# mLSTM cell and quick-gelu MLP on one core: the second product of the last chunk as three float32r products of 12-bit parts

## The chip, the cores and the metric

The kernel runs on one core of a Trainium2 chip. The metric is device time in microseconds of one launch, the median of several runs. Beside it there is one profiled execution with a trace of every instruction: its span is the time from the first instruction to the last. Engines are named as in the profile: PE (matmul) and PEld (its weight load), DVE (VectorE), ACT (ScalarE), POOL (GpSimd), SP (the queue that issues most DMAs).

## The reference, cut to what matters

The first part is an mLSTM recurrence over 768 steps for 4 batches and 8 heads of 40. Its output, turned to 3072 tokens by 320, goes through an MLP with 2048 hidden units:

```python
def _moe_ref(x, w_in, w_out) -> np.ndarray:      # x 3072 x 320
    h = x @ w_in                                  # w_in 320 x 2048
    g = h * (1.0 / (1.0 + np.exp(-1.702 * h)))
    return (g @ w_out).astype(np.float32)         # w_out 2048 x 320
```

Inputs and output are fp32.

## The kernel before

**Chunks.** The sequence is cut into NW = 6 chunks w of 128 steps. A chunk has 4 batches, so 512 tokens. For each chunk the kernel computes the recurrence in chunked form (`attention`, L967), then the first product with gelu, then the second product. The order of instructions is written out by hand in the loop over w (from L980); each engine takes its instructions in that order, and waits only for data and for buffers. While PE works on chunk w's second product, the recurrence of chunk w + 1 is put between its blocks through the table `side`.

**First product.** Chunk 0 uses plain fp32 (`up`, L645). Chunks 1 to 5 use `up_fast` (L789): inputs and weights are split into 12-bit parts, named high, low, diff and rest, and eight float32r matmuls of 128x128 by 512 tokens are summed for each of two hidden slices, j = 0 to 7. Four go to a bank called side, four to one called main. ACT copies side out of PSUM with a factor (L823), DVE joins main to it (L825), and ACT takes the gelu in place (L784) one j later. The result `gs[w, j]` holds 2 slices of 128 hidden units by 512 tokens. Even j take PSUM from two pairs of banks (`banks`, L356), odd j from four single ones.

The weight parts `w_diff` and `w_low` do not all fit in SBUF. In chunk 1 they are made and written to DRAM by `keep` (L728, on ACT's queue), and later chunks bring them back with `fetch_diff` and `fetch_low` (L749 to L754, on SP's queue) in the last blocks of the chunk before.

**Second product.** Chunk 0 uses `down` (L830): 64 fp32 matmuls with gelu outputs of 128 tokens as weights and 320 columns of `w_out` moving. Chunks 1 to 5 use `down_fast` (L876), one level of Strassen's scheme (Winograd's form) in fp32: two blocks of 128 tokens by the two halves of the hidden units by the two halves of the columns. There are 7 products of 8 matmuls with 160 columns for each of two pairs of token blocks, so 14 blocks of code and 112 matmuls (L889) instead of 64 with 320 columns. The token side needs sums of gelu outputs: `hidden_difference` and `hidden_sums` (L854 to L868, POOL and DVE) and `last_sums` (L870, DVE). The weight side needs `t1`, `t2`, `t4` and w11 - w01; `weight_sums` (L846, POOL) makes them once, and the last one overwrites `w01`, the right half of the first eight slices of `w_out_sb` (L93), in chunk 1 (L1035). DVE folds each product into the output tile (L892, L894), and SP stores it (L898).

**The loop's places that matter here.** In the loop over j of a chunk w > 0 (L1011 to L1053) each `up_fast(w, j)` is followed by `keep` and the weight splits (chunk 1), the next chunk's loads and transposes, `hidden_difference` from j = 2 or 3 on, and `hidden_sums` on POOL for j = 6 and 7. Then come the last gelu and `hidden_sums(w, (2, 3), V)` (L1057), and the blocks of the second product (L1065). In the last chunk there is no next chunk, so ACT, DVE and POOL have only the gelu chain and the sums.

Of the kernel before, what the change touches and what calls it, by code (L numbers as in the profile page):

```python
# [18 lines left out]
L = 128  # L19
# [12 lines left out]
def kernel(  # L32
# [44 lines left out]


    f_sb, i_sb = {}, {}
    k_st = const.tile([L, BH * D + DP - D], FP, name="k_st")  # L80
    q_sq = const.tile([L, BH // 2 * 4 * D + 32], FP, name="q_sq")
    k_sq = const.tile([L, BH // 2 * 4 * D + 32], FP, name="k_sq")
    t_sb = const.tile([128, 3, NH * DH], FP, name="t_sb")
    t1, t2, t4 = (t_sb[:, i, :].rearrange("p (f m) -> p f m", m=DH) for i in range(3))
    t_flat = t_sb.rearrange("p i x -> p (i x)")
    q_st, k_0, k_1 = (t[:, 0:BH * DP].rearrange("s (h d) -> s h d", d=DP) for t in (q_sq, k_sq, t_flat))
    at_bits, at_const = BH * DP, BH * DP + 1024
    v_st = const.tile([L, BH, D1], FP, name="v_st")
    eo = {}
    w_in = [win.tile([128, 2, 512], FP, tag="wa", name="w_in") for _ in range(3)]  # L90
    w_in.append(work.tile([128, 2, 512], FP, tag="wx", bufs=1, name="w_in"))
    w_in_x = work.tile([128, NF // 2, 128], FP, tag="xh", bufs=1, name="w_in_x")
    w_out_sb = const.tile([128, NF, DM], FP, name="w_out_sb")  # L93

    def load_gates(w):
        for dst, src in ((f_sb, f_gate), (i_sb, i_gate)):
# [43 lines left out]
    w_out_flat = w_out_sb.rearrange("p f m -> p (f m)")  # L140


    def piece_in(c, n):
# [7 lines left out]
    def piece_out(n):  # L151
        parts, c = [], n * 512
        while c < n * 512 + 512:
            f, m = divmod(c, DM)
            e = min(c + DM - m, n * 512 + 512)
            parts += [(slice(0, 128), slice(c - n * 512, e - n * 512), out_bits[:, f, 2 * m:2 * (m + e - c)])]
            c = e
        return w_out_flat[:, n * 512:(n + 1) * 512], parts

    pieces = []  # L160
    for n in range(4):
# [67 lines left out]
        G.memset(t[:, :, D:DP], 0.0)  # L229

    mark = const.tile([L, 1], FP, name="mark")
    state = [const.tile([128, BH // 2, D1], FP, name=f"state{i}") for i in range(2)]
    state_mid = const.tile([128, BH // 2, D1], FP, name="state_mid")

    m_at, ends = {0: m0}, {}
# [385 lines left out]
    def wait_for(x):  # L621

        G.tensor_copy(out=mark[0:x.shape[0]], in_=x[:, 0:1])
# [206 lines left out]
    def down(w, b, n):  # L830
        if n == 0:
            o_ps[w, b] = ps_m.tile([128, DM], FP, tag="m", name="p_out")
        po = o_ps[w, b]
        for f in range(n * 4, n * 4 + 4):
            T.matmul(po, gs[w, f // 2][:, f % 2, b * L:(b + 1) * L], w_out_sb[:, f, :], start=(f == 0),  # L835
                     stop=(f == NF - 1))
# [6 lines left out]
    w00, w01 = w_out_sb[:, 0:NH, 0:DH], w_out_sb[:, 0:NH, DH:DM]  # L843
    w10, w11 = w_out_sb[:, NH:NF, 0:DH], w_out_sb[:, NH:NF, DH:DM]
# [31 lines left out]
    def down_fast(w, c):  # L876
# [19 lines left out]
        def store(two):  # L896
# [8 lines left out]
                lambda: (product(block(1, 1), t4, (o10, o10)), store(1)),  # L905
                lambda: (product(total(2), w11, (o01, o01)), store(0))]


    def run(calls):
        for f, *args in calls:  # L910
            f(*args)
# [68 lines left out]
    for w in range(NW):  # L980
        more = w + 1 < NW
        if w == 0:
            for j in range(NF // 2):
                if j % 2 == 0:
                    ahead, behind = converted[j // 2]
                    if j:
                        run([(convert, p) for p in ahead])
                    run([(fetch, p) for p in fetched.get(j // 2, ())])
                    up(w, j, lambda: run([(columns_turn, 1) if p is None else (convert, p) for p in behind]), last_seam)
                if j == 6:  # L990
                    load(1, "o")
                if j == 1:
                    wait_for(w_in[1][:, 1, :])
                    scale(0, 1)
                    load(1, "v")
                if j < B and j % 2:
                    carry(0, j // 2)
                if j == 3:
                    masks()
                    gates(1)  # L1000
                    columns_in(1)
                if j == 4:
                    spread(1)
                    load_squares(1, "q")
                if j >= B:
                    transposes(1, j - B)
        else:
            if w == 1:
                split_diff(1)
                split_low(1, V)  # L1010
                more_rooms(1)  # L1011
            for j in range(NF // 2):
                up_fast(w, j)
                if more and j == 0:
                    gates(w + 1)
                if w == 1:
                    if j == 0:
                        split_high(2)
                    if j == 1:
                        for n in (0, 1):  # L1020
                            keep(w_diff_row, n, w_diff[1, n])
                        split_diff(2)
                        split_low(2, V)
                    if j == 2:
                        split_high(3)
                        keep(w_diff_row, 2, w_diff[1, 2])
                        keep(w_low_row, 2, w_low[1, 2])
# [21 lines left out]
                lag = 3 if w == 1 else 2  # L1049
                if lag <= j < 4 + lag:  # L1050
                    hidden_difference(w, j - lag)
                if j >= 6:
                    hidden_sums(w, (j - 6,), G)  # L1053
            gelu_fast(w, NF // 2 - 1)
            if more:
                load(w + 1, "o")
            hidden_sums(w, (2, 3), V)  # L1057
        side = attention(w + 1) if more else {}
        if more:
            rooms(w + 1)  # L1060
        if w == 0:

            blocks = [(lambda b=b, n=n: down(w, b, n)) for n0 in (0, 2) for b in range(B) for n in (n0, n0 + 1)]
        else:
            blocks = down_fast(w, 0) + down_fast(w, 1)  # L1065
        for i, block in enumerate(blocks):
            if w == 0 and i == 0:
                columns(1)
                convert_begin(17)
                weights_exp(1, 0)  # L1070
                fill_squares(q_sq)
                convert_end(17)
                for n in (1, 3, 5, 7):
                    block_transposes(1, n)
            if w == 0 and i in (4, 5):
                convert(14 + i)
            if w + 2 < NW and i == (6 if w == 0 else 0):
                load_gates(w + 2)
            if w == 0 and i == 13:
                load_squares(w + 2, "k")  # L1080
            if w == 0 and i == 15:
                load_squares(w + 2, "q")
            block()
            run(side.get(i, []))
            if w == 1 and i == 4:
                last_sums(1, 0, (2, 3))
            if w == 0 and i == 5:
                wait_for(w_out_flat[:, 9 * 512:])
                weight_sums(1)
                weight_sums(3)  # L1090
            if w == 0 and i == 5:
                split_high(0)
                split_rest()
                split_high(1)
            if w == 0 and i == 9:
                split_diff(0)
                split_low(0, V)
                split_rest_low()
            if w and more:
                if i == 11:  # L1100
                    fetch_diff(w + 1, (0, 1))
                    fetch_low(w + 1)
                    if w + 2 < NW:
                        load_squares(w + 2, "k")
                if i == 13:
                    fetch_diff(w + 1, (2, 3))
                    if w + 2 < NW:
                        load_squares(w + 2, "q")

# [29 lines left out]
```

## Time and profile before

| | us |
|---|---|
| three runs | 445.94, 448.19, 444.94 |
| median | 445.94 |
| the profiled execution's own time | 447.5 |
| its span | 445.8 |
| PE busy in it | 440.1 |
| last chunk, first product (chain, from 382.91) | 29.38 |
| last chunk, second product (chain, from 412.29) | 30.44 |
| from its end at 442.73 to the end of the span | 3.1 |

Times inside the span count from its start. In the chain of work that ended last, each piece is a start, a length, an engine, what it wrote, a line of the kernel and the number of records. A matmul in fp32 leaves two records in the trace, one in float32r leaves one. PE's records overlap, so the spacing of starts, or a piece's length over its count, tells what a matmul costs; the length of one record is longer.

### The profile page before, as it was taken

How to read it: one execution, taken by the hardware profiler on the slowest of the kernel's cores; microseconds unless marked ns; L12 is line 12 of the kernel's file. 1: busy time of each engine (PE TensorE's matmuls, PEld its weight loads, DVE VectorE, ACT ScalarE, POOL GpSimd, SP SyncE). 2: the span in 40 equal slices, each digit the busy share in tenths (PEclk: the TensorE clock that was granted, in tenths of full speed). 3: DMA queues.
4: the chain of work that ended last, by engine and by line, in shares of the span. 5: the costliest groups of instructions: out<-in, count | busy, mean ns of one | idle time of the engine just before them, and what ended most of it. 6: DMA issues, size and time to landing. Idle time of an engine off the chain costs nothing.

```text
span 445.8 us, 12211 instructions
## 1 busy us (share of the span) xinstructions
PE 440.1 (99%) x4999; PEld 384.0 (86%) x4999; DVE 327.3 (73%) x660; ACT 228.9 (51%) x494; POOL 130.8 (29%) x131
## 2 busy tenths in 40 slices
PE   8999999999999999999999999999999999999997
PEld 6867887776889999888999888999888999888997
DVE  4888999989999877778686779686769566634512
ACT  5677779902787701687701486800486900366000
POOL 6401327440066700135700034700035610035000
PEclk9999999999999999999999999999999999999999
DMA  8999999017777427979026978216988306600000
GB/s 168 196 283 165 242 271 216 2 35 196 183 200 161 63 63 218 267 111 168 13 59 188 270 102 176 44 34 143 328 114 156 61 19 151 232 31 0 1 31 29
DMA packets 129656, 60.06 MB, mean 135 GB/s; under 512 B 102096, under 2 KB 122528, under 8 KB 129600
## 3 DMA queue, kind: packets, MB, share of 16 engines
q1 hardware_dynamic: 120512, 54.86, 55.8%
q10 hardware_dynamic: 8768, 4.28, 3.3%
q8 instruction: 39, 0.64, 0.6%
q0 software_dynamic: 320, 0.15, 0.2%
q14 instruction: 17, 0.14, 0.1%
HBM read 49.10 MB, written 10.16 MB: 133 GB/s over the span
## 4 chain that ended last, share of the span: by engine, by line
PE 93%; SPq 4%; DMA 2%; DVE 1%; issue 0%; ACT 0%; DVEq 0%
PE p_out L889 34%; PE p L806 17%; PE p_h L806 16%; PE p_out L835 8%; PE p_h L657 7%; SPq L132 3%; PE p L534 2%; PE p L490 2%; PE p L542 2%; PE p L633 2%; PE p_h L666 2%; DMA bits<-in_moe_w_in_dram 2%; DVE state L610 0%; PE p L406 0%; DVE state_mid L642 0%
## 5 line engine op out<-in xcount | busy, mean ns | idle before, releaser
L857 POOL TENSOR_TENSOR g<-g 128x512 f32<-128x512 f32 x20 | 25.8, 1297 | 159.5 <-ACT g L784 159.5
L889 PE MATMUL p_out<-w_out_sb,g 128*128 128x160 f32 x480 | 68.9, 300 | 0.0
L889 PEld LDWEIGHTS p_out<-w_out_sb,g 128*128 128x128 f32 x480 | 66.4, 190 | 0.6
L765 ACT ACTIVATE x_high<-xT 128x512 fp32r<-128x512 f32 x10 | 6.3, 630 | 95.9 <-DVE xT L603 95.9
L894 DVE TENSOR_TENSOR o_sb<-o_sb,p_out 128x160 f32<-128x160 f32 x70 | 21.1, 318 | 44.8 <-PE p_out L889 44.7
L784 ACT ACTIVATE g<-g 128x512 f32<-128x512 f32 x80 | 46.4, 627 | 2.9 <-DVE g L825 2.6
L889 PE MATMUL p_out<-t_sb,s 128*128 128x160 f32 x320 | 47.1, 300 | 0.0
L825 DVE SCALAR_TENSOR_TENSOR g<-p,g 128x512 f32<-128x512 f32 x40 | 25.7, 681 | 27.3 <-PE p L806 12.8
L889 PEld LDWEIGHTS p_out<-t_sb,s 128*128 128x128 f32 x320 | 44.4, 190 | 0.2
L823 ACT ACTIVATE g<-p 128x512 f32<-128x512 f32 x40 | 21.7, 597 | 39.4 <-PE p L806 38.1
L463 ACT ACTIVATE wt<-wt,cols 128x64 f32<-128x64 f32 x160 | 38.9, 334 | 0.1
L835 PE MATMUL p_out<-w_out_sb,g 128*128 128x320 f32 x128 | 35.7, 436 | 0.0
L825 DVE SCALAR_TENSOR_TENSOR g<-p_h,g 128x512 f32<-128x512 f32 x40 | 26.4, 683 | 11.3 <-PE p_h L806 8.1
L835 PEld LDWEIGHTS p_out<-w_out_sb,g 128*128 128x128 f32 x128 | 23.9, 190 | 9.6
L657 PE MATMUL p_h<-xT,w_in 128*128 128x256 f32 x128 | 29.8, 385 | 1.1 <-ACT xT L574 1.1
L657 PEld LDWEIGHTS p_h<-xT,w_in 128*128 128x128 f32 x128 | 23.6, 190 | 6.4 <-issue 2.2
L823 ACT ACTIVATE g<-p_h 128x512 f32<-128x512 f32 x40 | 23.4, 595 | 10.2 <-PE p_h L806 10.2
L470 POOL TENSOR_SCALAR_AFFINE_SELECT wt<-wt 64x1024 f32<-64x1024 f32 x20 | 24.6, 1230 | 6.9 <-ACT wt L463 6.2
L806 PE MATMUL p_h<-x_diff,w_diff 128*128 128x512 f32 x80 | 25.1, 394 | 0.0
L806 PE MATMUL p<-x_rest,w_rest 128*128 128x512 f32 x80 | 25.1, 394 | 0.0
L806 PE MATMUL p_h<-x_rest,w_rest 128*128 128x512 f32 x80 | 25.0, 394 | 0.0
L806 PE MATMUL p<-x_diff,w_diff 128*128 128x512 f32 x80 | 25.0, 393 | 0.0
(206 smaller groups left out, 936.7 us busy)
## 6 DMA issues: line engine op xcount, KB each, us to landing
w_diff<-w_row SPq DMA_DIRECT2D x16, 512.0 KB, 4.8
wt<-m_row SPq DMA_DIRECT2D x20, 256.0 KB, 5.6
bits<-in_moe_w_in_dram SPq DMA_DIRECT2D x8, 512.0 KB, 10.0
out_dram<-o_sb SPq DMA_DIRECT2D x24, 160.0 KB, 3.1
q_sq<-in_q_dram SPq DMA_DIRECT2D x10, 320.0 KB, 8.6
eo<-in_o_gate_dram SPq DMA_DIRECT2D x5, 640.0 KB, 5.4
bits<-in_moe_w_out_dram SPq DMA_DIRECT2D x8, 320.0 KB, 5.7
q_sq<-x_row SPq DMA_DIRECT2D x10, 256.0 KB, 2.9
```

The costliest lines, as they stand in the source:

```text
L132: nc.sync.dma_start(out=dst[:, hs, 0:D], in_=src[bs, :, w * L:(w + 1) * L, :].rearrange("b h s d -> s (b h) d"))
L463: A.activation(out=x[:, h, :], in_=x[:, h, :], func=AF.Exp, scale=-1.0, bias=cols[w][:, c * PH + h:c * PH + h + 1])
L470: G.affine_select(out=r, in_=r, compare_op=OP.is_ge, fill=0.0, base=0, pattern=[[0, PH], [1, HL]], channel_multiplier=-1)
L657: T.matmul(ph[j][i][:, t], w_in[f // 4][:, c, f % 4 * 128:f % 4 * 128 + 128], x[:, c, t], start=(first and c == 0 and n == 0), stop=(not f ...
L784: A.activation(out=g, in_=g, func=AF.Gelu_apprx_sigmoid)
L806: T.matmul(dst[i], a(i), x, start=(first and m == which[0]), stop=(last and m == which[-1]))
L823: A.activation(out=g[:, i, :], in_=side[i], func=AF.Copy, scale=-BASE)
L825: V.scalar_tensor_tensor(out=g[:, i, :], in0=main[i], scalar=1.0 + 1.0 / BASE, in1=g[:, i, :], op0=OP.mult, op1=OP.add)
L835: T.matmul(po, gs[w, f // 2][:, f % 2, b * L:(b + 1) * L], w_out_sb[:, f, :], start=(f == 0), stop=(f == NF - 1))
L857: G.tensor_tensor(out=a10, in0=a00, in1=a10, op=OP.subtract)
L889: T.matmul(po, a(f), b[:, f, :], start=(f == 0), stop=(f == NH - 1))
L894: V.tensor_tensor(out=dst, in0=x, in1=po, op=OP.add)
```

## The change

It touches only the last chunk's second product, with what has to be prepared for it. In place of Strassen's scheme in fp32, gelu outputs g and weights w_out are split into a high part h of 12 bits (times 1 - 2^-13), a difference d = x - (1 + 2^-12) h, and a low part (x - h for g; 2^12 d + h for w_out). The three float32r products h.h, d.d and low.low are summed with factors: h.h and low.low in a main bank, d.d in a side bank. Gelu outputs of 128 tokens are the weights, 320 columns of the part of w_out move.

- `g_split` makes the three parts of a gelu tile for 128 tokens (one batch b): ACT the high part, DVE the difference, and POOL (b = 0) or DVE (b = 1 to 3) the low part. For b = 0 it is called in the up loop one j behind, for b = 1 after the last gelu, for b = 2 and 3 behind the products of b = 0 and 1.
- `out_part` makes the parts of w_out: two ACT calls of 1280 columns in chunk 4's blocks, two DVE calls ahead of the last up loop, and the rest between its j.
- `keep_w01` writes the original w01 to DRAM in chunk 1 (ACT's queue), before Strassen's sum overwrites it; `fetch_w01` brings it back after chunk 4's last block (SP's queue).
- `down_parts` runs the 48 matmuls of a batch, in the order of pairs 4, 5, 6, 0, 1, 2, 3, 7, then ACT copies the side bank out and DVE joins it with main.
- `w_out_sb` becomes two tiles of eight slices. Room for the parts comes from tiles that are no longer used: v_st, k_st, t_sb, q_sq, k_sq, the states, the second w_out tile, and buffers of kT, qT, wt and the pools.
- `hidden_difference`, `hidden_sums` and `down_fast` are not called for the last chunk.

```diff
+    def keep_w01():
+        w01_row.append(rows.tile([128, NH, DH], FP, tag="w01", bufs=1, name="w01_row"))
+        nc.scalar.dma_start(out=w01_row[0], in_=w01)
+
+    def fetch_w01():
+        nc.sync.dma_start(out=w01, in_=w01_row[0])
...
+    def out_part(part, f, n=4):
+        (h, at), (to, x) = wo[0, f], wo[part, f]
+        h, to, w = h[:, at:at + n], to[:, x:x + n], w_out_sb[f // NH][:, f % NH:f % NH + n]
+        if part == 0:
+            A.activation(out=to, in_=w, func=AF.Copy, scale=BIAS)
+        elif part == 1:
+            V.scalar_tensor_tensor(out=to, in0=h.bitcast(FP), scalar=-1.0 - 1.0 / BASE, in1=w, op0=OP.mult, op1=OP.add)
+        else:
+            d, at = wo[1, f]
+            V.scalar_tensor_tensor(out=to, in0=d[:, at:at + n].bitcast(FP), scalar=BASE, in1=h.bitcast(FP), op0=OP.mult,
+                                   op1=OP.add)
+
+    def g_split(j, b, engine):
...
+        h, d, low = (g_part[n, b, j] for n in range(3))
+        x = gs[NW - 1, j][:, :, b * L:(b + 1) * L]
+        A.activation(out=h, in_=x, func=AF.Copy, scale=BIAS)
+        V.scalar_tensor_tensor(out=d, in0=h.bitcast(FP), scalar=-1.0 - 1.0 / BASE, in1=x, op0=OP.mult, op1=OP.add)
+        engine.tensor_tensor(out=low, in0=x, in1=h.bitcast(FP), op=OP.subtract)
+
+    def down_parts(b):
+        both = banks("p_out")
+        main, side = both[:, 0, 0:DM], both[:, 1, 0:DM]
+        order = [f for j in pairs_out for f in (2 * j, 2 * j + 1)]
+        for f in order:
+            for n, dst in enumerate((main, side, main)):
+                T.matmul(dst, g_part[n, b, f // 2][:, f % 2], wo[n, f][0][:, wo[n, f][1]],
+                         start=(f == order[0] and n < 2), stop=(f == order[-1] and n > 0))
+        o = op.tile([128, DM], FP, tag="o", name="o_sb")
+        A.activation(out=o, in_=side, func=AF.Copy, scale=-BASE)
+        V.scalar_tensor_tensor(out=o, in0=main, scalar=1.0 + 1.0 / BASE, in1=o, op0=OP.mult, op1=OP.add)
+        t = (NW - 1) * L
+        nc.sync.dma_start(out=out[b * S + t:b * S + t + L, :], in_=o)
...
+            if not more:
+                room_out(1, 8, 4, "v_st", 1312)
+                room_out(1, 12, 4, "k_st", 1304)
+                out_part(1, 8)
+                out_part(1, 12)
...
                     if j == 0:
                         split_high(2)
+                        keep_w01()
...
+                if not more:
...
+                    run([(out_part, *x) for x in (((2, 8),), ((2, 12),), ((0, 0, 2), (0, 2, 2)),
+                                                  ((0, 4, 2), (0, 6, 2), (1, 0)), ((1, 4),), ((2, 0),),
+                                                  ((2, 4, 2), (2, 6, 2)), ())[j]])
+                    if j:
+                        g_split(j - 1, 0, G)
+                    continue
...
-            hidden_sums(w, (2, 3), V)
+            if more:
+                hidden_sums(w, (2, 3), V)
+            else:
+                g_split(NF // 2 - 1, 0, G)
+                for j in pairs_out:
+                    g_split(j, 1, V)
...
+            blocks = []
+            for b in range(B):
+                down_parts(b)
+                if b + 2 < B:
+                    for j in pairs_out:
+                        g_split(j, b + 2, V)
...
+                if w + 2 == NW and i == 8:
+                    room_out(0, 8, 8, "k_sq", 2592)
+                    out_part(0, 8)
+                    out_part(0, 12)
                 if i == 13:
                     fetch_diff(w + 1, (2, 3))
+                    if w + 2 == NW:
+                        fetch_w01()
```

More of the change, by code (lines that the diff above doesn't have):

```diff
@@ L79 @@
     f_sb, i_sb = {}, {}
[L80 to L83, printed above, removed]
+    k_st = const.tile([L, BH * D + DP - D], FP, tag="k_st", name="k_st")
+    q_sq = const.tile([L, BH // 2 * 4 * D + 32], FP, tag="q_sq", name="q_sq")
+    k_sq = const.tile([L, BH // 2 * 4 * D + 32], FP, tag="k_sq", name="k_sq")
+    t_sb = const.tile([128, 3, NH * DH], FP, tag="t_sb", name="t_sb")
     t1, t2, t4 = (t_sb[:, i, :].rearrange("p (f m) -> p f m", m=DH) for i in range(3))
@@ L87 @@
     at_bits, at_const = BH * DP, BH * DP + 1024
-    v_st = const.tile([L, BH, D1], FP, name="v_st")
+    v_st = const.tile([L, BH, D1], FP, tag="v_st", name="v_st")
     eo = {}
@@ L92 @@
     w_in_x = work.tile([128, NF // 2, 128], FP, tag="xh", bufs=1, name="w_in_x")
-    w_out_sb = const.tile([128, NF, DM], FP, name="w_out_sb")
+    w_out_sb = [const.tile([128, NH, DM], FP, tag=f"w_out{i}", name=f"w_out{i}") for i in range(2)]
     def load_gates(w):
@@ L138 @@
     out_bits = w_out_bits.rearrange("(f p) m -> p f m", p=128)
-    w_out_flat = w_out_sb.rearrange("p f m -> p (f m)")
+    w_out_flat = [x.rearrange("p f m -> p (f m)") for x in w_out_sb]
     def piece_in(c, n):
@@ L157, in piece_out @@
             c = e
-        return w_out_flat[:, n * 512:(n + 1) * 512], parts
+        return w_out_flat[n // 5][:, n % 5 * 512:(n % 5 + 1) * 512], parts
     pieces = []
@@ L231 @@
     mark = const.tile([L, 1], FP, name="mark")
-    state = [const.tile([128, BH // 2, D1], FP, name=f"state{i}") for i in range(2)]
+    state = [const.tile([128, BH // 2, D1], FP, tag=f"state{i}", name=f"state{i}") for i in range(2)]
     state_mid = const.tile([128, BH // 2, D1], FP, name="state_mid")
@@ L834, in down @@
         for f in range(n * 4, n * 4 + 4):
-            T.matmul(po, gs[w, f // 2][:, f % 2, b * L:(b + 1) * L], w_out_sb[:, f, :], start=(f == 0),
+            T.matmul(po, gs[w, f // 2][:, f % 2, b * L:(b + 1) * L], w_out_sb[f // NH][:, f % NH, :], start=(f == 0),
                      stop=(f == NF - 1))
@@ L840, in down @@
             nc.sync.dma_start(out=out[b * S + w * L:b * S + (w + 1) * L, :], in_=o)
-    w00, w01 = w_out_sb[:, 0:NH, 0:DH], w_out_sb[:, 0:NH, DH:DM]
-    w10, w11 = w_out_sb[:, NH:NF, 0:DH], w_out_sb[:, NH:NF, DH:DM]
+    (w00, w01), (w10, w11) = ((x[:, :, 0:DH], x[:, :, DH:DM]) for x in w_out_sb)
     def weight_sums(n):
@@ L906, in down_fast, with room_out @@
                 lambda: (product(total(2), w11, (o01, o01)), store(0))]
+    w01_row = []
+    pairs_out = (4, 5, 6, 0, 1, 2, 3, 7)
+    wo, g_part = {}, {}
+    def keep_w01():
[3 more added lines that the diff above has]
+        nc.sync.dma_start(out=w01, in_=w01_row[0])
+    def room_out(part, f, nf, tag, n):
+        t = const.tile([128, n], FR, tag=tag, name="w_part")
+        t = t[:, 0:nf * DM].rearrange("p (f m) -> p f m", m=DM)
+        wo.update({(part, f + x): (t, x) for x in range(nf)})
@@ new lines, in g_split @@
+    def g_split(j, b, engine):
+        if b % 2 == 0 and (0, b, 0) not in g_part:
+            for part, name in ((0, "kT"), (1, "qT")):
+                for n in range(4):
+                    t = work.tile([128, 2, 2, L], FR, tag=name, bufs=4, name=name)
+                    g_part.update({(part, b, 2 * n + x): t[:, x] for x in range(2)})
+        if (2, b, j) not in g_part:
+            j0 = j // 4 * 4
+            for part in range(3) if b % 2 else (2,):
+                if part == 2:
+                    pool, tag, n = (win, "wb", 3) if b % 2 else (work, "wt", 2)
+                    t = pool.tile([128, 4, 2, L], FR, tag=tag, bufs=n, name="g_part")
+                else:
+                    t = sp.tile([128, 4, 2, L], FR, tag="g", name="g_part")
+                g_part.update({(part, b, j0 + x): t[:, x] for x in range(4)})
+        h, d, low = (g_part[n, b, j] for n in range(3))
[3 more added lines that the diff above has]
+        engine.tensor_tensor(out=low, in0=x, in1=h.bitcast(FP), op=OP.subtract)
@@ L1049 @@
                 lag = 3 if w == 1 else 2
+                if not more:
+                    if j == 0:
+                        room_out(2, 8, 12, "t_sb", 3840)
+                        wo.update({(2, f): (wo[2, 8][0], 8 + f) for f in range(4)})
+                    if j == 2:
+                        room_out(0, 0, 8, "w_out1", 2560)
+                    if j == 3:
+                        room_out(1, 0, 8, "q_sq", 2592)
+                    if j == 6:
+                        room_out(2, 4, 2, "state0", 656)
+                        room_out(2, 6, 2, "state1", 656)
+                    run([(out_part, *x) for x in (((2, 8),), ((2, 12),), ((0, 0, 2), (0, 2, 2)),
[4 more added lines that the diff above has]
+                    continue
                 if lag <= j < 4 + lag:
@@ L1056 @@
                 load(w + 1, "o")
-            hidden_sums(w, (2, 3), V)
+            if more:
+                hidden_sums(w, (2, 3), V)
+            else:
+                g_split(NF // 2 - 1, 0, G)
+                for j in pairs_out:
+                    g_split(j, 1, V)
         side = attention(w + 1) if more else {}
@@ L1063 @@
             blocks = [(lambda b=b, n=n: down(w, b, n)) for n0 in (0, 2) for b in range(B) for n in (n0, n0 + 1)]
-        else:
-            blocks = down_fast(w, 0) + down_fast(w, 1)
+        elif more:
+            blocks = down_fast(w, 0) + down_fast(w, 1)
+        else:
+            blocks = []
[4 more added lines that the diff above has]
+                        g_split(j, b + 2, V)
         for i, block in enumerate(blocks):
@@ L1087 @@
             if w == 0 and i == 5:
-                wait_for(w_out_flat[:, 9 * 512:])
+                wait_for(w_out_flat[1][:, 4 * 512:])
                 weight_sums(1)
```

## The prediction, on record before the changed kernel ran

> **What bounds the kernel now.** I read the page's busy shares first, then the chain in order of time, then the matmuls one by one, then DVE, ACT and the DMA around the last chunk.
>
> From the page:
>
> ```profile
> PE 440.1 (99%) x4999; PEld 384.0 (86%) x4999; DVE 327.3 (73%) x660; ACT 228.9 (51%) x494; POOL 130.8 (29%) x131
> PEclk9999999999999999999999999999999999999999
> ```
>
> PE is busy for 440.1 of 445.8 us at the full granted clock, so only PE's own time, the start and the tail can move the end. The chain in order of time (start, length, what) shows the stage that changes:
>
> ```profile
> 66.40 8.62 PE p_out L835 x32
> ...
> 408.62 3.67 PE p_h L806 x16
> 412.29 30.44 PE p_out L889 x224
> 442.73 0.02 issue
> 442.76 0.32 DVE o_sb L894
> ```
>
> The last second product is one unbroken PE run of 30.44 us. The program has 112 matmuls there and the chain counts 224: an fp32 matmul is two records, each 30.44 / 224 = 135.9 ns for 160 columns. L835, also fp32, has 8.62 / 32 = 269.4 ns a record for 320 columns. L806 is float32r, 16 matmuls and 16 records: 3.67 / 16 = 229.4 ns for 512 columns in one record. The timeline of PE (start, length of two merged, name) gives starts of L806:
>
> ```profile
> 408.46 0.62 PE L806 MATMUL p_h<-x_rest,w_rest 128*128 128x512 f32 x2
> 408.92 0.63 PE L806 MATMUL p_h<-x_diff,w_diff 128*128 128x512 f32 x2
> ...
> 410.31 0.62 PE L806 MATMUL p_h<-x_high,w_high 128*128 128x512 f32 x2
> 410.77 0.62 PE L806 MATMUL p_h<-x_low,w_low 128*128 128x512 f32 x2
> 411.22 0.62 PE L806 MATMUL p_h<-x_high,w_high 128*128 128x512 f32 x2
> ```
>
> Starts of pairs are 0.46 us apart for rest and diff (410.31 - 408.46 over 8: 231 ns each) and 0.455 for high and low (411.22 - 410.31 over 4: 227.5 ns). The other engines in the two stretches (DVE, ACT, POOL busy in the third to fifth number):
>
> ```profile
> 382.90:412.30 29.40, 29.40 (x131) 24.05 (x130) 11.96 (x21) 17.79 (x32) 10.35 (x8) 1.00 0.16 55
> 412.30:442.70 30.40, 30.40 (x224) 30.18 (x223) 10.42 (x28) 1.17 (x2) 0.00 (x0) 1.00 0.05 17
> ```
>
> In the first product of the last chunk DVE has 17.4 us free, ACT 11.6. That is the cover for the new splitting.
>
> **The change, part by part.**
>
> *The product itself (on the path).* Removed: 224 records, 30.44 us. Added: 4 blocks of 128 tokens x 16 slices x 3 products = 192 float32r matmuls of 320 columns. No such row exists, so I bound it. From 160 to 320 columns an fp32 record grows by 269.4 - 135.9 = 133.5 ns, two passes over 160 columns, so one pass over 320 columns costs 133.5 ns, and an fp32 record has 135.9 - 133.5 = 2.4 ns beyond its passes. One pass over 512 columns is 213.6 by the same slope, so float32r has 229.4 - 213.6 = 15.8 ns beyond its pass: 13.9 for high and low, 17.4 for rest and diff. Low end: 2.4 ns as in fp32, pitch 135.9, 192 x 0.1359 = 26.1 us. Middle: the excess grows with the columns, 229.4 x 320 / 512 = 143.4, 27.5 us. If it is a fixed sum per matmul: high and low 147.4, diff 150.9, mean (147.4 x 2 + 150.9) / 3 = 148.6, 28.5 us. High end: each matmul waits for its own weight load, whose record is 188 ns at L806 and 190 at L889; 192 x 0.190 = 36.5 us. I take 148.6: nothing in the rows of fp32 lets the excess grow with columns, and loads of 190 ns are hidden at a 135.9 ns pitch in L889. Product: 28.5 - 30.44 = -1.9 us.
>
> A row against a rule: the pitch just read is 229.4 ns at 512 columns. The Trainium skill ("TensorE: Matmul & The Clock Gate", Back-to-back issue gap) gives N / 2.4 + 2.5 ns, 215.8 at 512 and 135.8 at 320; the fp32 records agree with it and the float32r records do not. By that rule the product would take 26.1 us, the low end, and the change would gain 3.9 us instead of 1.5; by the rows it is 28.5.
>
> *The end (on the path).* Before: the last fold, DVE 0.32 us, then the store. After: ACT copies the side bank (128x320 from PSUM, L839 0.425 us), DVE joins it with the main bank (128x320, L509 0.49). The side bank closes one matmul (0.15) before the end: 0.425 + 0.49 + 0.04 - 0.15 = 0.80 against 0.35. +0.45 us. The store is of the same 160 KB.
>
> *Splitting the gelu outputs.* Per slice pair and block of 128 tokens: ACT 128x256 (L766, 0.40), DVE twice 128x256 (L773 and L874, 0.42 each). Block 0 goes into the up loop with its subtraction on POOL (half of L857's 1.295, 0.65; the removed hidden differences and sums there were 10.35 us, the new ones 8 x 0.65). Blocks 1 to 3: DVE 8 x 0.84 + 0.49 for the join = 7.2 us a block at most, against PE's 48 x 0.1486 = 7.13. DVE has a lead: from the timeline of DVE,
>
> ```profile
> 408.71 1.29 DVE L825 SCALAR_TENSOR_TENSOR g<-p,g 128x512 f32<-128x512 f32 x2 [2.97 <-PE p L806]
> 411.48 0.69 DVE L825 SCALAR_TENSOR_TENSOR g<-p_h,g 128x512 f32<-128x512 f32 x1 [1.48 <-ACT g L823]
> 412.40 0.69 DVE L825 SCALAR_TENSOR_TENSOR g<-p_h,g 128x512 f32<-128x512 f32 x1 [0.23 <-PE p_h L806]
> ```
>
> its last join of the first product ends at 413.1, and PE needs block 1 only at 412.3 + 7.1 = 419.4. Block 1 is split by 414.8 + 6.7 = 421.5, its last pair needed at 425.7; block 3 by about 436, needed from 433.7 to 439.9, its first pair ready at 430. Cost nothing, cover 4 us. The tight place is pair 6 of block 0: after 410.0 DVE has two halves of weight parts (0.82 each) and one split (0.42), so its joins run 412.1 to 413.3 and the difference of pair 6 is ready at 413.7; PE reads it as the 14th matmul, 412.3 + 13 x 0.1486 = 414.2. Nothing, with 0.5 us in hand.
>
> *Splitting w_out.* DVE: 128x1024 takes 1.22 (L720) and 128x512 0.69, so 128x1280 is 1.48 and 128x640 0.82. Seven and two of them plus six 128x256: 10.4 + 1.6 + 2.5 = 14.5, to 26.5 of 29.4 us. ACT: 4 x 0.73 (from 0.63 for 512 and 1.25 for 1280, L394) + 7 x 0.40 = 5.7, to 23.5 of 29.4. Behind these wait the copies and joins that empty PSUM; each pair of banks is needed again only two slice pairs (7.3 us) later, and I find them at most 1.1 us late. The two ACT parts in chunk 4's last blocks (2 x 1.25) lie where the timeline of ACT is empty, from 373.4 to 378.04. Nothing. The two DVE parts after chunk 4 end at 384.9 + 2 x 1.42 = 387.7, and the next join, 387.31 before, comes 0.4 late: nothing, by the same slack.
>
> *Keeping and bringing back w01.* Writing it out in chunk 1 puts one DMA of 655 KB on ACT's queue ahead of w_diff's. Neighbours of 512 KB took 0.34 to 0.45 us to issue; PE then waits for ACT's copies only when their bank returns at 120.75. The DMA windows there:
>
> ```profile
> 116.00:120.00 4.00, 4.00 (x19) 3.29 (x18) 3.77 (x16) 3.95 (x6) 0.00 (x0) 1.00 0.69 266
> 120.00:126.00 6.00, 6.00 (x28) 4.91 (x27) 6.00 (x8) 5.93 (x11) 0.00 (x0) 1.00 0.36 22
> ```
>
> 655 KB at 266 GB/s is 2.5 us, and it delays the first two w_diff rows into the slack stretch, before the next rows move at 127. POOL's sum that overwrites w01 began at 126.6, so it waits for nothing. Bringing it back is the last of SP's loads (w_diff landed at 391.8); it lands near 394.4, when ACT first reads it (after the gelus that ended at 394.3). Behind it SP has only stores. Nothing, up to 1 us of ACT's slack.
>
> *Sum.* 445.8 - 30.44 + 28.5 + 0.45 = 444.3 us of span, -1.5. The profiled execution took 447.5 us in all, 0.35% above the median of 445.94 us; the same ratio (0.9967) on the median gives 444.5.
>
> **The rivals.**
> 1. Less excess per matmul: pitch 143.4 gives 443.4, pitch 135.9 gives 442.0. For it: fp32 records of the same column count. Against: every float32r row. The Trainium skill's rule quoted above leads here.
> 2. The weight load becomes the bound, and the end is slower. Place: each of the 192 matmuls; price at a pitch of 190 ns: 36.5 - 30.44 + 0.45 = +6.5, 452.4 us. It decides from a pitch of (30.44 - 0.45) / 192 = 156.2 on. For it: every float32r load seen had 224 ns or more of matmul over it, so a hidden load at 150 has not been shown. Against: in L889 fp32 loads of 190 ns follow each other every 136. The Trainium skill (same page, LDWEIGHTS) gives columns / 1.2, 107 ns for 128; even so it would fit under 133.
> 3. A part comes late: pair 6's difference by more than 0.5 us, or w01's return after 395. PE then stands for the shortfall; 1 to 2 us eat the gain: about 446.
> 4. float32r at 320 columns gives no saving in passes: excluded by L806, one record of 229 ns at 512.
>
> **How the numbers follow.** Forecast 0.62; rival 1, 0.18; rival 3, 0.12; rival 2, 0.06; 0.02 for a wait I did not find. The range 442.0 to 447.0 holds the forecast, rival 1 and rival 3 with the scatter of the three runs (444.94 to 448.19), and leaves out rival 2. About 1% (4.5 us) is what a measurement of this kernel can tell from no change. Faster by over that needs a pitch under (30.44 - 0.45 - 4.46) / 192 = 133.0 ns, below the bare pass: 0.02. Slower by over that needs 179.5 ns: rival 2 and the unfound wait, 0.08. Within: 0.90.
>
> **What would show it.** The chain's last PE piece should read x192 and about 28.5 us, with pair starts 0.295 to 0.30 apart. A piece of 26.1 is rival 1; loads that end right where the next matmul starts, at 160 ns or more, rival 2; DVE, ACT or DMA pieces in the chain between 412 and 441, rival 3. The start of that piece should stay within 0.3 us of 412.3; a later one means that the up loop or chunk 1 pays for the splitting, and my prediction of covered work is wrong.

## The result, and the profile after

| | before | after |
|---|---|---|
| median of six runs each, us | 446.67 | 452.73 |
| range of the runs | 444.94 to 448.19 | 451.03 to 454.69 |
| ratio, 95% interval | | 1.0139 (1.0103 to 1.0174) |
| profiled execution, us | 447.5 | 451.03 |
| its span | 445.8 | 449.3 |

The changed kernel is 1.4% slower, outside the predicted range of 442.0 to 447.0. (One execution of before_three and one of side_first ran over 1.5% above the fastest of their kernel and are left out of the times below; that of before_three is the profiled one, so its span is not compared.)

The page after, its first line and the two rows of 40 slices that answer to those shown of before:

```profile
PE 437.5 (97%) x4967; PEld 381.2 (85%) x4967; DVE 349.7 (78%) x701; ACT 245.6 (55%) x536; POOL 128.7 (29%) x131
PE   8999999999959999999999999999999999999996
PEclk9999999999998999999999999999999999999999
```

PE did 2.6 us less work (437.5 against 440.1), and yet the span is longer. The 5 in the twelfth slice and the 8 of the clock in the thirteenth (11.2 us each) lie between 124 and 146 us, in chunk 1. The change was aimed at the last chunk, at 410. So the chain is read at both places. First the last chunk (start, length, what):

```profile
413.38 3.68 PE p_h L806 x16
417.06 28.19 PE p L963 x192
...
445.27 0.45 ACT o_sb L966
...
445.74 0.49 DVE o_sb L967
```

The product takes 28.19 instead of 30.44 us, in one unbroken piece: 28.19 / 192 = 146.8 ns a matmul. The end behind it, to 446.23, takes 0.98 instead of 0.35. Together -1.62 us. But the piece begins at 417.06 instead of 412.29, 4.77 later.

PE's waits of the whole program, longest first (line, tile, what released it; total, times, longest):

```profile
PE p L806 <- ACT g L823: 5.0, 1, 5.0
PE p_idle L207 <- DVE one L213: 1.1, 1, 1.1
```

The first wait is new. The chain of chunk 1's first product shows its place:

```profile
118.80 3.69 PE p_h L806 x16
...
133.71 1.09 ACT g L823 x2
...
134.84 5.34 PE p L806 x16
140.18 3.67 PE p_h L806 x16
```

The chain leaves PE after pair 3 and follows SP and ACT; PE ran pairs 4 and 5 beside them until 129.82. Then it waits for ACT's copies (L823) to give slice pair 6 its banks, and the pair takes 5.34 instead of 3.67 us. The stretches of the two pairs give the reason (length, busy time of PE, PEld, DVE, ACT, POOL, then the granted clock):

```profile
134.84:140.18 5.34, 5.33 (x17) 4.33 (x18) 5.34 (x8) 4.85 (x10) 3.29 (x3) 0.71 1.04 204
140.18:143.80 3.62, 3.62 (x18) 2.95 (x17) 3.62 (x6) 2.13 (x5) 3.18 (x3) 1.00 0.89 110
```

Over the pair behind the 5.0 us wait the granted clock is 0.71: 0.50 from 134.47 to 137.87, then 1.00 again. PE worked 3.0 us of that stretch at half clock and lost 1.5 us by it, most of the 1.67. From the first to the last matmul start of the eight pairs, chunk 1's first product takes 36.02 us, before 29.31: +6.71 = 5.0 + 1.67 and a rest of 0.04. In the profiled executions after also began chunk 0's first product 1.95 us earlier (24.11 against 26.06; among all profiled executions it lies between 23.5 and 26.2, for reasons not looked into); 6.71 - 1.95 = 4.76, the shift of the last piece.

Why ACT copied late is in ACT's timeline (start, length of two merged, what; in brackets the idle time before it and its releaser). After:

```profile
121.40 0.44 ACTq L730 DMA_DIRECT2D w_row<-w_low  x1
...
122.92 1.15 ACT L784 ACTIVATE g<-g 128x512 f32<-128x512 f32 x2
130.94 0.33 ACTq L730 DMA_DIRECT2D w_row<-w_diff  x1
131.36 1.04 ACT L734 CAST w_low<-w_low 128x1024 fp32r<-128x1024 f32 x1 [7.28 <-DMA v_st<-in_v_dram]
132.43 1.25 ACT L118 COPY q_sq<-q_sq 32x512 f32<-32x512 f32 x2
133.71 1.09 ACT L823 ACTIVATE g<-p 128x512 f32<-128x512 f32 x2
```

And before, the same instructions:

```profile
123.36 0.44 ACTq L730 DMA_DIRECT2D w_row<-w_low  x1
...
125.32 0.33 ACTq L730 DMA_DIRECT2D w_row<-w_diff  x1
...
126.51 1.06 ACT L734 CAST w_low<-w_low 128x1024 fp32r<-128x1024 f32 x1 [0.48 <-DVE w_low L726]
...
129.99 1.09 ACT L823 ACTIVATE g<-p 128x512 f32<-128x512 f32 x2 [1.13 <-PE p_h L806]
```

The last w_diff row, `keep(w_diff_row, 3, ...)`, is issued 2 us behind the row before it in the kernel before, and 9.5 us behind it after. ACT stood 7.28 us in front of it, and the release is put down to a DMA with which the row shares no data: a load of v on SP's queue. In the trace that load landed at 130.86 and the row was issued at 130.94.

What the two share is a semaphore. Each DMA of SP and ACT signals its landing on one of a set of semaphores; the records here show eight in use, handed out anew again and again. The program as built names them, 0 to 7, and makes a DMA wait for the earlier DMA that holds its semaphore. Three DMAs of either kernel as the built program lists them, the second load of v (SP) and the last two rows (ACT):

```
before  L130 v_st<-in_v_dram 64x16x40     [waits DMAHW7, PE]
before  L730 w_row<-w_low    128x1024     [waits DMAHW6]
before  L730 w_row<-w_diff   128x1024     [waits DMAHW1, DVE]
after   L130 v_st<-in_v_dram 64x16x40     [waits DMAHW6, PE]
after   L730 w_row<-w_low    128x1024     [waits DMAHW0]
after   L730 w_row<-w_diff   128x1024     [waits DMAHW6, DVE]
```

After, the last row draws number 6, which the second load of v holds: issued at 120.38, landed 10.5 us later. Before, it drew number 1, last held by a small DMA that had landed at 121.22.

### The profile page after: what moved, and what is told of

Its sections match the earlier page's. It is cut to its first block, busy times and chain, and to the rows that moved or that the text cites. A ratio compares the mean times of both kernels' runs of the same rounds, so it can differ in the third digit from the quotient of the medians.

```text
span 449.3 us, 12223 instructions
## 1 busy us (share of the span) xinstructions
PE 437.5 (97%) x4967; PEld 381.2 (85%) x4967; DVE 349.7 (78%) x701; ACT 245.6 (55%) x536; POOL 128.7 (29%) x131
## 4 chain that ended last, share of the span: by engine, by line
PE 80%; DVE 6%; SPq 6%; DMA 5%; issue 1%; ACT 1%; DVEq 0%
PE p_out L888 27%; PE p L806 16%; PE p_h L806 16%; PE p L963 6%; PE p_out L835 3%; PE p_h L657 3%; SPq L132 3%; PE p L534 2%; PE p L542 2%; PE p L490 2%; DMA bits<-in_moe_w_out_dram 2%; PE p L633 1%; DMA wt<-m_row 1%; DMA bits<-in_moe_w_in_dram 1%; DVE qT L415 1%
## 5 line engine op out<-in xcount | busy, mean ns | idle before, releaser
L856 POOL TENSOR_TENSOR g<-g 128x512 f32<-128x512 f32 x16 | 20.6, 1292 | 125.5 <-ACT g L784 125.5
L888 PE MATMUL p_out<-w_out,g 128*128 128x160 f32 x384 | 55.2, 300 | 0.0
L888 PEld LDWEIGHTS p_out<-w_out,g 128*128 128x128 f32 x384 | 53.1, 190 | 0.5
L823 ACT ACTIVATE g<-p 128x512 f32<-128x512 f32 x40 | 21.7, 596 | 35.3 <-PE p L806 35.2
L893 DVE TENSOR_TENSOR o_sb<-o_sb,p_out 128x160 f32<-128x160 f32 x56 | 16.7, 315 | 28.4 <-PE p_out L888 28.4
L888 PE MATMUL p_out<-t_sb,s 128*128 128x160 f32 x256 | 37.8, 301 | 0.0
L835 PE MATMUL p_out<-w_out,g 128*128 128x320 f32 x128 | 35.7, 436 | 0.0
L888 PEld LDWEIGHTS p_out<-t_sb,s 128*128 128x128 f32 x256 | 35.5, 190 | 0.2
L835 PEld LDWEIGHTS p_out<-w_out,g 128*128 128x128 f32 x128 | 23.9, 190 | 9.6
L806 PE MATMUL p<-x_rest,w_rest 128*128 128x512 f32 x80 | 26.1, 408 | 5.0 <-ACT g L823 5.0
L823 ACT ACTIVATE g<-p_h 128x512 f32<-128x512 f32 x40 | 23.3, 595 | 8.8 <-PE p_h L806 8.8
L806 PE MATMUL p<-x_diff,w_diff 128*128 128x512 f32 x80 | 25.6, 401 | 0.0
L806 PE MATMUL p_h<-x_diff,w_diff 128*128 128x512 f32 x80 | 25.1, 394 | 0.0
L806 PE MATMUL p_h<-x_rest,w_rest 128*128 128x512 f32 x80 | 25.0, 394 | 0.0
```

The source lines that it names most:

```text
L806: T.matmul(dst[i], a(i), x, start=(first and m == which[0]), stop=(last and m == which[-1]))
L823: A.activation(out=g[:, i, :], in_=side[i], func=AF.Copy, scale=-BASE)
L856: G.tensor_tensor(out=a10, in0=a00, in1=a10, op=OP.subtract)
L888: T.matmul(po, a(f), b[:, f, :], start=(f == 0), stop=(f == NH - 1))
L893: V.tensor_tensor(out=dst, in0=x, in1=po, op=OP.add)
```

## The experiments

Theory 1: the added DMA costs nothing by its bytes. It shifts the hand-out, so that the last row waits, in ACT's in-order queue, for an unrelated long load; the copies behind it come late, PE stands, and its clock drops. Theory 2: the 655 KB themselves are the cost, by what they take from the DMA engines at a busy time. Each kernel was timed in the same rounds as the kernel before; ratios are to that.

**no_keep** leaves out writing w01 aside and bringing it back, so the last product uses overwritten weights.

```diff
                         split_high(2)
-                        keep_w01()
...
-                    if w + 2 == NW:
-                        fetch_w01()
```

> The changed kernel without the DMA that writes w01 out in chunk 1 and the one that brings it back; the last chunk then uses Strassen's difference in place of w01, so that part of the output is another one. All theories that put the loss on this DMA expect chunk 1 without a stall, chunk 5's second product at 28.2 us and a time of 446.7 - 1.8 = 444.9 us (ratio 0.996). If the loss is elsewhere (the earlier stages, the split tile of w_out, the splitting work), it stays near 452.

Measured: 444.73 us, ratio 0.9962 (0.9940 to 0.9983). PE's new wait is gone, chunk 1's first product takes 29.31, and the end of the chain reads:

```profile
409.70 28.19 PE p L963 x192
...
437.92 0.45 ACT o_sb L966
```

The whole loss comes from the DMA that sets w01 aside or its return; everything else gives about what was forecast for the whole.

**keep_7of8** keeps and brings back only seven of the eight slices of w01 at the same place, so one slice of weights is overwritten.

```diff
-        nc.scalar.dma_start(out=w01_row[0], in_=w01)
+        nc.scalar.dma_start(out=w01_row[0][:, 0:7], in_=w01[:, 0:7])
...
-        nc.sync.dma_start(out=w01, in_=w01_row[0])
+        nc.sync.dma_start(out=w01[:, 0:7], in_=w01_row[0][:, 0:7])
```

> The changed kernel with 7 of 8 slices of w01 written out and brought back (573 of 655 KB), at the same place; the eighth slice stays Strassen's difference. In the listing of waits the last row of w_diff now draws the semaphore of the first load of v, which landed at 127.2 us, not that of the second (130.9). Theory 1: ACT is held until about 127.2, 3.7 us less; PE waits 5.0 - 3.7 = 1.3 us and keeps its clock, about 446.5 us. Theory 2: seven eighths of the loss stay, about 451.5 us.

Measured: 445.86 us, ratio 0.9979 (0.9963 to 0.9996). In this build the row stands one place earlier in the hand-out and draws the semaphore of the first load of v (number 5), which landed at 127.40; the row was issued at 127.47. ACT's wait of the stretch, and the longest of PE at L806:

```profile
ACT w_low L734 <- DMA v_st<-in_v_dram: 3.3, 1, 3.3
```

```profile
PE p L806 <- ACT g L823: 1.0, 1, 1.0
```

Seven eighths of the bytes cost a fifth of the delay (first product 30.64, +1.33): not the bytes, but whose landing the row waits for. The granted clock behind this 1.0 us wait was 1.00; the pair still took 3.97 instead of 3.67 us, and what costs this 0.30 was not found.

**before_three** adds to the kernel before, without any of the change, three DMAs of 1280 bytes on ACT's queue ahead of the last row.

```diff
+    def extra(n):
+        for i in range(n):
+            to = rows.tile([1, DM], FP, tag=f"x{i}", bufs=1, name="extra_row")
+            nc.scalar.dma_start(out=to, in_=w_out_sb[0:1, NF - 1, :])
...
+                        extra(3)
                         keep(w_diff_row, 3, w_diff[1, 3])
```

> The kernel before with three DMAs of 1280 bytes put on ACT's queue just ahead of the last row of w_diff in chunk 1, nothing else changed. In the listing of waits that row now draws the semaphore of the second load of v (landing at 133.3 us in the trace of before). Theory 1: the row is issued at 133.3 instead of 125.3, ACT stands for 8 us, its copies of slice pair 4 come at about 136, PE waits some 5 us and loses some 1.7 more at the lower clock: about 453 us. Theory 2: 4 KB move nothing, 446.7 us.

Measured: 451.96 us (median of three), ratio 1.0128 (1.0095 to 1.0161). The row now draws number 7, that of the second load of v in this kernel (landed 136.01, row issued 136.09). ACT's and PE's waits:

```profile
ACT w_low L734 <- DMA extra_row<-w_out_sb: 6.1, 1, 6.1
```

```profile
PE p L806 <- ACT g L823: 3.7, 1, 3.7
```

ACT's wait is put down to one of the small DMAs, the last of which itself went out only at 133.63; but what came last before the row's issue was the load of v. Pair 6 then takes 6.64 us at a granted clock of 0.56, and chunk 1's first product 36.10 (+6.79, after +6.71). Less than 4 KB in the old kernel cost as much there as the whole change: theory 2 falls.

**early_keep** issues the full 655 KB earlier, on the same queue, behind block 9 of chunk 0's second product.

```diff
+                keep_w01()
...
                         split_high(2)
-                        keep_w01()
```

> The same bytes of w01 written out in chunk 0's second product (behind its block 9) instead of chunk 1. Theory 1 (eight completion semaphores are handed out in turn, and the added DMA makes the last row of w_diff on ACT's queue draw the one that a slow load of v still holds): that row draws another one here, ACT issues it without a wait, PE has no stall in chunk 1, about 444.9 us. Theory 2 (the 655 KB hold back the rows behind them on ACT's queue in chunk 1): also 444.9, since the bytes are gone from there. A theory in which the DMA costs wherever it stands: about 450 or more.

Measured: 446.32 us, ratio 0.9985 (0.9966 to 1.0004). The row draws another number (2), and the wait at pair 6 is gone (29.31). A new one stands at the start of chunk 1:

```profile
PE p L806 <- ACT x_high L765: 1.6, 1, 1.6
```

The 655 KB, issued at 100.62 and landed at 106.16, lie over the last three of the small reads that bring the next chunk's x into SBUF; the first of these three took 5.0 us (102.07 to 107.09), against 2.7 in no_keep (101.55 to 104.23). Both theories had put this kernel at 444.9, 1.4 us lower, since neither looked at this place. So bytes do cost something here, where a short chain of transfers is what PE waits for.

**keep_at_start** puts the full DMA between these two places: first on ACT's queue in chunk 1.

```diff
+                keep_w01()
             for j in range(NF // 2):
                 up_fast(w, j)
...
-                        keep_w01()
```

> The changed kernel with all 655 KB of w01 written out on ACT's queue in chunk 1 as before, but as its first DMA (ahead of slice pair 0 instead of behind it). In the listing of waits the last row of w_diff then draws the semaphore of a small row of m that lands at about 121 us. Theory 1: the row is issued without a wait at about 123.5, no stall of PE at slice pair 4, about 445.0 us (up to 1 us more if the bytes delay the loads of q beside them). Theory 2 (bytes ahead of the rows on ACT's queue): the stall of 5 us stays, about 452.5.

Measured: 444.88 us, ratio 0.9957 (0.9933 to 0.9982). The DMA ran from 108.50 to 113.83, the row drew number 2 and went out in time, chunk 1's first product takes 29.34, and the last chunk is as after:

```profile
410.80 28.19 PE p L963 x192
...
439.01 0.45 ACT o_sb L966
...
439.49 0.49 DVE o_sb L967
```

This is the change as it was meant, with all its work and bytes, and 0.4% faster than before: one line moved is worth 1.8%.

**keep_pool** gives the same DMA to POOL's queue instead, which leaves the hand-out of SP and ACT as it was before.

```diff
-        nc.scalar.dma_start(out=w01_row[0], in_=w01)
+        nc.gpsimd.dma_start(out=w01_row[0], in_=w01)
```

> The changed kernel with the write of w01 issued by POOL at the same place in the code; nothing else changed. In the listing of waits DMAs of POOL draw from another set of semaphores, and every row of w_diff has the one that it has in the kernel before. Theory 1: no stall in chunk 1, 446.7 - 1.8 = 444.9 us, as without the DMA. Theory 2: the same bytes in the same stretch, some 5 us of stall, 451 to 452.5 (less if POOL issues them earlier than ACT did).

Measured: 449.23 us, ratio 1.0043 (1.0015 to 1.0071): the forecast was missed. The wait at pair 6 is gone as expected (29.32). But POOL had nothing ahead of the DMA and issued it as soon as its sum before it was done:

```profile
94.05 0.90 POOL L914 DMA_DIRECT2D w_row<-w_out  x1
```

It landed at 98.69, over the writes of x at the end of chunk 0, and PE waits 0.8 us for `x_high` in this profile, which is of the fastest run (446.67). The next kernel issues the same DMA, and its profile shows more of it:

```profile
PE p L806 <- ACT x_high L765: 3.0, 1, 3.0
```

There the first four writes of x took 2.9 to 4.5 us, in no_keep 1.7 to 2.1. The wait ends at 110.84, the granted clock is 0.50 from 110.42 to 113.81, and chunk 1's first product takes 30.64, +1.33. 3.0 + 1.33 is 4.3 us, about the distance of both medians from no_keep's (449.2 and 449.0 against 444.7). What I had left out: ACT's queue had also held the DMA back to a harmless time. That the bytes slow the writes is read from the overlap; a smaller DMA was not tried here.

**side_first** is keep_pool, with the last block's 16 side matmuls ahead of its main ones, so that ACT's copy of the side bank could run beside them.

```diff
-        for f in order:
-            for n, dst in enumerate((main, side, main)):
+        steps = [(f, n) for f in order for n in range(3)]
+        if b == B - 1:
+            steps = [(f, 1) for f in order] + [(f, n) for f in order for n in (0, 2)]
```

> keep_pool, and in the last block of 128 tokens all 16 matmuls of the side bank run ahead of the 32 of the main bank, so that ACT's copy lies under PE. The end after the last matmul should fall from 0.96 us (ACT 0.45, DVE 0.49, two steps of 0.02) to 0.51: 0.45 us under keep_pool, about 444.4 us. If DVE waits for something else there, as keep_pool.

Measured: 449.02 us, ratio 1.0032 (1.0001 to 1.0063), and no gain at the end:

```profile
415.00 28.19 PE p L965 x192
443.19 0.02 issue
443.21 0.45 ACT o_sb L968
```

ACT still starts 0.02 us behind PE's last matmul, although the side bank was done 32 matmuls earlier. Side and main are halves of one tile; the likely reading is that the copy waits for the last writer of the whole tile, and the next kernel tries it.

**two_banks** is keep_at_start with that order in the last block, and side and main in two tiles of one bank.

```diff
+        if b == B - 1:
+            side, main = (bank("p_out")[:, 0:DM] for _ in range(2))
+            steps = [(f, 1) for f in order] + [(f, n) for f in order for n in (0, 2)]
+        else:
+            both = banks("p_out")
```

> Keep_at_start (w01 kept aside at the start of chunk 1, 444.88 us, no PE stall) with one more edit: the last block of 128 tokens accumulates its main and its side product in two separate tiles of one bank each, and all 16 side matmuls run ahead of the 16 main ones. Theory: in side_first ACT's copy of the side product waited for the last writer of a tile that holds both halves, so it began 0.02 us after PE's last matmul. With two tiles the copy (0.45 us) runs beside the 16 main matmuls (16 x 146.8 ns = 2.35 us), and only DVE's add (0.49 us) stays behind PE: the end goes from 0.96 to 0.51 us, 444.4 us in all. Rival: the two single banks come free later than the pair did, PE waits for one of them ahead of the last block, and the gain is given back: 444.9 us or more, with a PE wait at the second product's line in the listing of waits.

Measured: 444.74 us, ratio 0.9962 (0.9945 to 0.9978). The chain's end:

```profile
430.80 7.05 PE p_out L967 x48
...
437.93 0.49 DVE o_sb L971
```

ACT is off the chain, and from PE's last matmul to DVE's end it takes 0.57 instead of 0.99 us. The step is confirmed in the trace; 0.4 us is too little for the times to tell this kernel from keep_at_start.

**after_again** is the changed kernel, unedited, in the same rounds as two_banks.

> The changed kernel as it is, on the same chip and in the same rounds as two_banks. Theory: the 5.0 us wait of PE for ACT's copies and the slower slice pair behind it come back, 451 to 454 us, about 8 us above two_banks. Rival: the loss was a matter of the chip that measured it, and the changed kernel comes within 2 us of two_banks here.

Measured: 453.31 us, ratio 1.0142 (1.0111 to 1.0172), 8.6 us above two_banks. The same wait of 5.0 us is there, with the row issued at 130.48 and the load of v landed at 130.41. The hand-out is fixed when the program is built, so the loss comes back in each run.

**columns_160** is keep_pool with each matmul of 320 columns cut into two of 160 (a single run).

```diff
-                T.matmul(dst, g_part[n, b, f // 2][:, f % 2], wo[n, f][0][:, wo[n, f][1]],
-                         start=(f == order[0] and n < 2), stop=(f == order[-1] and n > 0))
+                for x in range(2):
+                    m = slice(x * DH, x * DH + DH)
+                    T.matmul(dst[:, m], g_part[n, b, f // 2][:, f % 2], wo[n, f][0][:, wo[n, f][1], m],
+                             start=(f == order[0] and n < 2 and x == 0), stop=(f == order[-1] and n > 0 and x == 1))
```

> keep_pool with every float32r matmul of 320 columns cut into two of 160 (384 matmuls, same columns in all). If float32r costs a fixed 13.5 ns beyond its pass, the pitch is 66.7 + 13.5 = 80.2 ns and the piece 384 x 0.0802 = 30.8 us, 2.6 more than 28.2. If the excess grows with the columns, 73.4 ns and 28.2 us. If the weight load of 128 columns bounds at this length, a pitch well over 80, up to the 188 ns of its record: 72 us.

Measured: 462.91 us, and the piece of the chain:

```profile
414.22 42.86 PE p L965 x384
```

42.86 / 384 = 111.6 ns, more than the 66.8 of a pass over 160 columns with the 13.3 found below. PE did not stand between them, so something below the matmul's own length paces it. That it is the weight load, one for each matmul, is the likely reading and was not tried by itself. The Trainium skill ("TensorE: Matmul & The Clock Gate", LDWEIGHTS) gives columns / 1.2, 107 ns for 128 columns; the run's 111.6 lies within 5 ns of it.

This run also shows the wait for `x_high` at the start of chunk 1 once more:

```profile
PE p L806 <- ACT x_high L765: 2.5, 1, 2.5
```

The granted clock behind it is 0.50 from 110.43 to 113.83.

## Why the prediction was wrong, step by step

- *The product itself*: right. Forecast 28.5 us at 148.6 ns, measured 28.19 at 146.8. A pass over 320 columns is 133.5, so the excess is 13.3 ns; high and low at 512 columns show about the same (226.6 to 227 ns from start to start in the last chunk of the kernel before, less 213.6). That fits a fixed sum per matmul, and rival 1, in which it would shrink with the columns (143.4) or to the 2.4 of fp32 (135.9), is out. Diff here does not carry the 17.4 that I had read from rest and diff in the first product: the next start follows high, diff and low after 146.3, 146.8 and 147.3 ns on average.
- *The end*: +0.63 instead of +0.45. I let the side bank close one matmul early; side_first showed that the copy waits for the whole tile, and two_banks that a tile of its own lifts this.
- *Splitting the gelu outputs* and *Splitting w_out*: right, covered. No wait of PE lies in the last chunk, and its last piece is unbroken, in every run. (The two parts of w_out that follow chunk 4 took 2.88 us together.)
- *Keeping and bringing back w01*: this is the step that failed. I put it at "Nothing", from the DMA's bytes and from what ACT and SP issue behind it. The bytes were harmless there, as far as keep_7of8 shows, and w01's return held ACT for 0.29 us (399.32) and PE not at all; but the step did not ask which landing each later DMA on the same queues waits for before it can be issued. The runs show 7.3 us of ACT's time in its place, which became 5.0 us of waiting on PE and 1.67 in the pair behind it, most of that by the lower clock: +6.7.
- *Sum*: -1.5 forecast. Without the failed step it is -1.62 in the trace (28.19 + 0.98 - 30.44 - 0.35), and -1.7 in the time of no_keep (0.38% of 446.7). With it: -1.62 + 6.71 = +5.1, where the medians give +6.1, with 4.6 to 7.8 by the interval. In both profiles of the changed kernel the profiled run was the fastest of its six. The mean clocks on record tell where the last 1 us may lie: 0.995 in the profiled run, 0.992 in the other five. A second stretch of 3.4 us at half clock behind the wait, as before_three's trace has it (0.50 from 139.03 to 145.84), would lower the mean by 0.004 and cost another 1.7 us, 452.7 in all. This is an estimate; no trace of the changed kernel shows that stretch.
- *Rivals*: rival 2, the weight load as bound, has a real floor, if columns_160 is rightly read, but at 112 ns, under the 146.8 that 320 columns need. Rival 3 named w01's return; it is not late. What happened was in the 0.02 for "a wait I did not find".
- *What would show it*: I had written that a later start of the last piece would mean that the up loop or chunk 1 pays. It did start later (4.77 us), and chunk 1 pays; not for the splitting, though.

The sign was in the trace of before. SP's waits there list issues held up by landings of other tiles (L130 loads v and k):

```profile
SPq L130 <- DMA q_sq<-in_q_dram: 2.1, 3, 0.8
...
SPq L130 <- DMA w_diff<-w_row: 1.1, 2, 0.7
```

The loads share no data with q_sq or w_diff. Such a line says that an issue can be tied to a landing by something other than data, and that adding one DMA may tie others.

## What to carry to other kernels

A DMA added to a queue can cost more than its bytes: where a few completion semaphores are handed out in turn, as here, it changes which earlier landing later DMAs wait for before they can be issued, and on an engine that also computes, that wait stands in front of its work. So look in the built program at what each issue on such an engine waits for, and if one waits for a long load, move the new DMA by a few instructions; before moving it to an idle queue, ask what had been holding it back. Two results that are ready at different times belong in separate tiles; in one tile, the reader of the first waited here for the last writer of both.

## What the runs showed of the hardware

- Eight completion semaphores are shared by the DMAs of SP and ACT in this program, and an issue follows the landing of the DMA that holds its semaphore by 0.07 to 0.08 us (130.86 to 130.94, 127.40 to 127.47, 136.01 to 136.09, 130.41 to 130.48).
- Waits of PE of 5.0 us (after, after_again), 3.0 (side_first) and 2.5 (columns_160) each came with 3.4 us at a granted clock of 0.50, which began between 0.4 us before the end of the wait and 0.7 us after it; behind waits of 1.6 (early_keep), 1.0 (keep_7of8) and 0.8 us (keep_pool) it stayed at 1.00. The Trainium skill ("TensorE: Matmul & The Clock Gate", HAM oscillation) names gaps of over about 3.4 us as what lowers the clock; the waits of 3.0 and 2.5 us are shorter, and the clock fell there too, so here the measurement decides. Where the bound lies, these runs leave open.
- A float32r matmul in one pass took the time of its columns plus about 13 ns, at 320 columns (146.8 ns) and for the high and low parts at 512 (226.6 to 227 ns; rest and diff there took about 231); at 160 columns the pitch was 111.6 ns, where this sum gives 80.
